# Two products behind a gated attention on one core: block 0 passes all six weight units before block 1, the plan's DMA costs and the addresses of the matmul operands change

## The chip, the core and the metric

The kernel runs on one core of a Trainium2 chip. A core has TensorE (PE, matmuls), VectorE (DVE), ScalarE (ACT), GpSimd (POOL) and SyncE (SP, which here issues nearly all DMAs). Each engine runs its own instructions in order and waits for others on semaphores. SBUF is the on-chip memory of 128 partitions, PSUM the accumulators that PE writes. The metric is the device time of one execution in microseconds, lower is better.

## The reference

```
def attention(q, k, v, alpha):              # B, H, S, D = 4, 8, 768, 48
    state = zeros(B, H, D, D)
    for t in range(S):
        state = alpha[:, :, t, :, None] * state + einsum('bhd,bhe->bhde', k[:, :, t], v[:, :, t])
        y[:, :, t] = einsum('bhd,bhde->bhe', q[:, :, t], state)
    return y

x = attention(...).transpose(0, 2, 1, 3).reshape(3072, 384)
x = ((x @ w_a) * (x @ w_b)) @ w_out         # 384 -> 1536 -> 384
h = x @ w_in                                # 384 -> 2048
return (max(h, 0) + beta * min(h, 0)) @ w_out2      # -> 384
```

Attention's inputs and beta are float32. The weights are float64; the chip reads them as 64-bit words and makes its own parts of them.

## The kernel before

**Work and tiling.** The 3072 tokens are 24 chunks of 128 (index g), four chunks make a block of 512 tokens (index n, 0 to 5). A block's attention result x is a tile of 512 columns, held as a high and a low part (both float32r, the format that PE takes at one column a cycle). The weights are likewise split into high and low. So each product is three matmuls: high by high, low weight by high x, high weight by low x (`mm3`, lines 926, 927, 929).

The first product has six units (index u) of 256 hidden columns, each in two halves (index i = 2u + o). A half-unit of a block is `up` for w_a (9 matmuls into tile pa), `up` for w_b (9 into pb), on ACT a copy of pa to a_sb, on DVE a_sb times pb (line 1057), on ACT the high part gh (line 950), on DVE the low part gl (line 954), and two half-units later `down1` with w_o (9 matmuls into acc). The second product has 8 units and 16 half-units a block: 9 matmuls into pi, DVE for the activation, gh and gl again, 9 matmuls into acc.

**Weights.** Each raw tile (ra, rb, ro; 768 KB) is loaded once and split by `conv`: five DVE operations of 768 columns and two ACT ones for each of the tiles, ending with line 453. Unit 0's tiles go partly over PE (the cl matmuls, lines 481 to 483). The second product's 16 tiles (ws) are split the same way between 200 and 430 us, stored to DRAM (w2d), and loaded back when SBUF is free.

**Attention.** Per chunk: loads of alpha (ra), of k and q (kq) and of v; on DVE two scans (lines 584 and 594, with a reciprocal of four values between them, line 590) that turn alpha into running products and their inverses, and the product kq times these (line 599); on PE scores (line 625), the chunk's own and cross terms (786, 808, 793); DVE and ACT move the state and x. The scans need a constant of ones and zeros as second operand: `ones` for the first, `invs` for the second, whose heads the reciprocal overwrites. From block 2 on (`BY_BLOCKS`) the keys are turned by DVE and by DRAM: `turn` (line 660) transposes 32 x 32 squares into kt, four DMAs store it to ktd (`away`, line 664), four load it back as ks (`back`, line 674). Kt and ks share one buffer (tag ks).

**What sets the order.** Operations are first entered in a graph with a duration, a latency and a key, and then ordered for all engines by a planner (`Graph.place`, `latest`, `search`): a list scheduler with a random search over the keys; its result is the order in which the instructions are written. The keys come from `at`, the planned start of each half-unit in the order of `SEGMENTS`, and for chunks of later blocks from `block_at[n] - (BC - c) * 12000 - 14000` in nanoseconds. `SEGMENTS` lists (block, first unit, end unit): blocks 0 and 1 pass units 0 to 2 each, then units 3 to 5 each, then the other blocks pass six. Where a block is left half-way its sums are copied to a tile part by ACT and added later by DVE (`evict1`). `SPLIT` names the (block, unit) whose matmuls are cut into two halves of 256 columns, so that they can start when two chunks are there. `fill` writes idle matmuls (wp) into planned gaps at the beginning.

**Addresses.** Tiles are laid out pool by pool in the order in which the pools are opened. The program has weights at 192 and x, gh and gl at 256 bytes past a multiple of 512.

Of the kernel before, what the change touches and what calls it, by code (L numbers as in the profile page):

```python
# [14 lines left out]
F32 = mybir.dt.float32  # L15
BF16 = mybir.dt.bfloat16
# [4 lines left out]
ALU = mybir.AluOpType  # L21
# [4 lines left out]
P = 128  # L26
CH = 128
HC = CH // 2
BC = 4
MB = BC * CH  # L30
SQ = 32
BT = P // SQ

SEGMENTS = (
    (0, 0, 3), (1, 0, 3), (0, 3, 6), (1, 3, 6),
    (2, 0, 6), (3, 0, 6), (4, 0, 6), (5, 0, 6),
)
LAG = 2
SPLIT = ((0, 0), (1, 0))
BY_BLOCKS = 2  # L40

ON_PE = (("a", 0), ("b", 0), ("o", 0))

# [2 lines left out]
HOP = 250  # L46
LEAD = {"DVE": 80, "ACT": 90}
T_MOE = 30000
STRETCH = 1.2
URGENT = 40000  # L50
PAUSE = 500
SLACK = 500
# [16 lines left out]
class Graph:  # L69
# [11 lines left out]
    def add(self, eng, dur, fn, key, deps=(), lat=0, after=(), pool=None, burst=False, line=None):  # L81
        o = Op()
        o.pool, o.hold, o.burst = pool, [], burst
        o.eng, o.dur, o.fn, o.key, o.lat = eng, dur - LEAD.get(eng, 0), fn, key, lat + LEAD.get(eng, 0)
        o.users, o.soft, o.n = [], [], len(self.ops)
        for d in {x.n: x for x in deps if x is not None}.values():
            d.users.append(o)
        for d in {x.n: x for x in after if x is not None}.values():
            d.soft.append(o)
        if line:  # L90
            if line in self.last and self.last[line] not in [x for x in after if x is not None]:
                self.last[line].soft.append(o)
            self.last[line] = o
        self.ops.append(o)
        return o
# [203 lines left out]
def body(tc, akq, v, vg, w_a, w_b, w_o1, w_in, w_o2, beta, out):  # L299
    nc = tc.nc  # L300
# [5 lines left out]
    NJ = H // 2  # L306
    D = KT * P // H
    GR = 64 - D
    NA = NJ * (CH + 1) + 1
    NC = NJ * CH  # L310
    NB = NG // BC

    with ExitStack() as ctx:
        ctx.enter_context(tc.manual_schedule())
        pool = lambda name, bufs=1, **k: ctx.enter_context(tc.tile_pool(name=name, bufs=bufs, **k))
        const, wpool, pers = pool("const"), pool("wpool"), pool("pers")
        xpool, cpool, gpool, tp = pool("xpool", 2), pool("cpool", 2), pool("gpool", 2), pool("tp", 2)
        dram = pool("dram", space=DRAM)
        ps_mm, ps_acc = pool("ps_mm", 2, space=PSUM), pool("ps_acc", space=PSUM)
        ps_att = pool("ps_att", space=PSUM)  # L320
# [4 lines left out]
        ident = plus.bitcast(F32)  # L325
        mask = const.tile([P, P], F32, name="mask")
        betaT = const.tile([P, F2], F32, name="betaT")
        ones = pers.tile([P, NJ, CH + 1], F32, name="ones")
        invs = pers.tile([P, NJ, CH + 1], F32, name="invs")
        Z = pers.tile([P, BC, NJ, D], F32, name="Z")  # L330
        At = pers.tile([P, 2 * NC], F32, name="As")
        x2d = [dram.tile([P, 2, KT, MB], F32, name=f"x2d{n}") for n in range(NB)]
        w2d = [dram.tile([P, 2 * UC], F32, name=f"w2d{i}") for i in range(2 * NU2)]
        ktd = [dram.tile([SQ, NJ, BT, P], F32, name=f"ktd{g}") for g in range(NG)]


        warm = ones.bitcast(BF16)[:, 0, 2 : 2 + 2 * CH]

        def fill(t0, t1):
            wp = ps_mm.tile([P, MB // 2], F32, name="wp", tag="mm")  # L340
            for _ in range(int((t1 - t0) * 0.7) // 110):
                nc.tensor.matmul(wp, warm[:, 0:P], warm, start=True, stop=True)

        nc.gpsimd.memset(ones, 0.0)
        nc.gpsimd.memset(ones[:, :, 0:1], 1.0)
        nc.gpsimd.memset(invs, 0.0)
        make_identity(nc, eye)
        nc.gpsimd.memset(mask, 1.0)
        nc.gpsimd.affine_select(
            out=mask, in_=mask, pattern=[[1, P]], compare_op=ALU.is_ge, fill=0.0,  # L350
# [10 lines left out]
        whole, parts = slice(0, MB), (slice(0, MB // 2), slice(MB // 2, MB))  # L361
        flat = [(n, 2 * u + o, s, t) for s, (n, u0, u1) in enumerate(SEGMENTS) for u in range(u0, u1)
                for t in (parts if (n, u) in SPLIT else (whole,)) for o in range(2)]
        span = lambda t: MM if t == whole else MM // 2 + 10
# [4 lines left out]
        due, block_at = {}, {}  # L369
# [131 lines left out]
        for u in range(NU1):  # L501
            for nm, src in (("a", w_a), ("b", w_b), ("o", w_o1)):
                x = nm, u
# [16 lines left out]
        st = [dict() for _ in range(NG)]  # L520
        xt, xuse, xdone, xpart = {}, {}, {n: [] for n in range(NB)}, {}
        xring, lring, rring, vring = Ring(2), Ring(2), Ring(2), Ring(2)
        aring, kring, sring = Ring(1), Ring(1), Ring(1)
        both = ps_att.tile([P, 2, 2 * NC // 2], F32, name="both")
        yfree, afree = [], []
        att = lambda nm: ps_att.tile([P, NJ, CH], F32, name=nm, tag="att")
        before = {"scan": None}
        accfree = [[] for _ in range(KT)]
        state = [[] for _ in range(BC)]
        sums = [At[:, NC + i * NJ * D : NC + (i + 1) * NJ * D].rearrange("p (j d) -> p j d", d=D) for i in range(2)]  # L530
        slots = [Z[:, c] for c in range(BC)] + sums[1:]

        def place(g):
            n, c = divmod(g, BC)
            key = c * 1000 - 100000 if n == 0 else block_at[n] - (BC - c) * 12000 - 14000
            if n == 1:
                key = block_at[n] - (BC - c) * 9500 - 6000

            def A(eng, dur, fn, deps, early=0, lat=0, after=(), line=None):
                return G.add(eng, dur, fn, key - early, deps, lat, after, burst=eng == "PE", line=line)  # L540

            return st[g], n, c, n == 0, A

        def inputs(g):
            s, n, c, start, A = place(g)
# [28 lines left out]
            kT = lambda: s["kq"][:, 0]  # L574
            qT = lambda: s["kq"][:, 1]
            r0 = lambda: s["ra"][:, 0 : NA - 1].rearrange("p (j t) -> p j t", j=NJ)[:, :, 0:1]
            la = A("SP", 1000 if g == 0 else 720, load_a, rwait, 14000, 2400 if g == 0 else 3000, line="ra")
# [5 lines left out]
            def scan_r():  # L583
                nc.vector.tensor_tensor_scan(
                    out=s["ra"][:, 0 : NA - 1][:, ::-1], data0=s["ra"][:, : NA - 1 : -1],
                    data1=ones.rearrange("p j t -> p (j t)"), initial=0.0, op0=ALU.mult, op1=ALU.add,
                )

            def recip():
                nc.vector.reciprocal(invs[:, :, 0:1], r0())  # L590

            def scan_a():
                a = s["ra"][:, NA - 1 : 2 * NA - 2]
                nc.vector.tensor_tensor_scan(out=a, data0=a, data1=invs.rearrange("p j t -> p (j t)"),
                                             initial=0.0, op0=ALU.mult, op1=ALU.add)

            def mul():
# [1 line left out]
                nc.vector.tensor_tensor(out=s["kq"], in0=s["kq"], in1=f[:, :, :, 1:], op=ALU.mult)  # L599

            turned = n >= BY_BLOCKS
            r = A("DVE", 1220, scan_r, [la])
            rc = A("DVE", 180, recip, [r, before["scan"]])
            sa = before["scan"] = A("DVE", 1220, scan_a, [rc])
            slack = SLACK if not start else 0
            k1 = q1 = A("DVE", 1220, mul, [lq, sa], 0, slack)
            rhold.append(k1)
# [33 lines left out]
        def chunk(g):  # L641
            s, n, c, start, A = place(g)
# [3 lines left out]
            kT, qT, r0, r, k1, lv = (s[x] for x in ("kT", "qT", "r0", "r", "k1", "lv"))  # L646
            spare, rhold, lhold, slack = (s[x] for x in ("spare", "rhold", "lhold", "slack"))
            ahead = st[g + 1] if n > 1 and g + 1 < NG else None
            turned = n >= BY_BLOCKS

# [5 lines left out]
                slots[c], slots[BC] = new, old  # L656

            def turn():
                s["kt"] = tp.tile([P, NJ, P], F32, name="kt", tag="ks", bufs=1)
                nc.vector.transpose(s["kt"], kT())  # L660

            def away(b):
                def f():
                    nc.sync.dma_start(
                        ktd[g].rearrange("t j a f -> t (j a) f")[:, :, b * SQ : (b + 1) * SQ],
                        s["kt"][b * SQ : (b + 1) * SQ].rearrange("p j (a d) -> p (j a) d", d=SQ),
                    )
                return f

            def back(a):  # L670
                def f():
                    if a == 0:
                        s["ks"] = tp.tile([P, NJ, P], F32, name="ks", tag="ks", bufs=1)
                    nc.sync.dma_start(s["ks"][a * SQ : (a + 1) * SQ], ktd[g][:, :, a, :])
                return f

            if turned:
                x = A("DVE", 650, turn, [k1, *kring.take()])
                lhold.append(x)
                moved = [A("SP", 430, away(b), [x], 0, 2000) for b in range(BT)]  # L680
                x = None
                back_at = []
                for a in range(BT):
                    x = A("SP", 350, back(a), moved, 0, 3800, after=[x])
                    back_at.append(x)

            zs = None
# [16 lines left out]
            if start:  # L704
# [3 lines left out]
                x = A("PE", 560, s["keys"], [k1, *w0])  # L708
                pa = A("PE", 1120, s["scores"], [k1, *w1, *w2])
            elif "front" in s:  # L710
                x = pa = s["front"]
            elif turned:
                x = pa = A("PE", 630, s["both"], [k1, *afree, *yfree])
            else:
                x = pa = A("PE", 1150, s["both"], [k1, *aring.take(), *afree, *yfree])
                khold = aring.last()
            if turned:
                ks = back_at
            else:
                ks = [A("ACT", 600, ev_k, [x, *kring.take()])]  # L720
# [131 lines left out]
            if start:  # L852
# [3 lines left out]
                x = A("ACT", 360, kept, [ds])  # L856
# [175 lines left out]
        def down1(k):  # L1032
            n, i, s, t = flat[k]
            _, u0, u1 = SEGMENTS[s]
            key = at[k + LAG] + 18 * MM
# [6 lines left out]
        for k, (n, i, s, t) in enumerate(flat):  # L1042
            u, o = divmod(i, 2)
            x = lambda n=n: xt[n]
            b = {}
# [31 lines left out]
        for k in range(2 * NU2):  # L1077
            b = {}
            key = t0 + k * (t1 - t0) // (2 * NU2)
            _, c = conv((w_in, w_o2)[k % 2][k // 2], f"s{k % 2}", f"s{k % 2}", key,  # L1080
                        [stored[k - 2]] if k >= 2 else part_users[k], lambda r, b=b: b.update(r=r))
# [10 lines left out]
        for k in range(2 * NU2):  # L1092
            x = "id"[k % 2], k // 2
# [55 lines left out]
        for k, (n, i) in enumerate(flat2):  # L1149
# [3 lines left out]
            b = {}  # L1153
            p, m, bh = up(at2[k], [done["i", u], ld], lambda n=n: xt[NB + n], ("i", u), o)
# [95 lines left out]
```

## Time and profile before

| | us |
|---|---|
| median of 3 runs | 943.03 |
| lowest, highest | 941.46, 948.37 |
| the profiled execution | 943.25 |
| its span, first to last instruction | 941.5 |
| PE busy in the span | 932.5 |
| DVE busy | 564.0 |
| ACT busy | 245.2 |

Matmuls overlap, so PE's busy time says that it nearly always has one under way, not that it is at its peak. What one matmul costs is the distance from its start to the next one's. An engine's idle time in a window is the window less its busy time.

### The profile page before, as it was taken

The page shows a single profiled execution, that of the slowest core. Times are in us where ns is not written, and L with a number is a line of the kernel's source. Part 1 is how long each engine was busy: PE and PEld are TensorE (multiplying, and loading weights), DVE is VectorE, ACT ScalarE, POOL GpSimd, SP SyncE. Part 2 cuts the span into 40 slices and gives each one's busy share as a digit, 9 for nine tenths or more (in the row PEclk, how much of TensorE's full clock was granted, in tenths as well). Part 3 has the DMA queues.
Part 4 walks back from the last instruction along what each step waited for, and adds up shares of the span by engine and source line. Part 5 has one row for each costly group of instructions (what it writes and reads, how often), then busy time and mean ns, then how long its engine had stood idle before and what let it go on. Part 6 is the DMA issues. An engine that isn't in the chain of part 4 may idle for free.

```text
span 941.5 us, 15646 instructions
## 1 busy us (share of the span) xinstructions
PE 932.5 (99%) x6637; PEld 760.1 (81%) x6637; DVE 564.0 (60%) x865; ACT 245.2 (26%) x406; POOL 2.2 (0%) x11
## 2 busy tenths in 40 slices
PE   9999999999999999999999999999999999999998
PEld 7788887888888788787888888888888888888886
DVE  8999964674886687663232264554545545545554
ACT  3555531223333333331122121111111111111111
POOL 0000000000000000000000000000000000000000
PEclk9999999999999999999999999999999999999999
DMA  9973103563657767763266620100200200200000
GB/s 353 403 262 102 32 1 79 159 189 137 210 162 228 249 207 217 241 175 93 82 235 202 212 91 1 68 34 1 89 12 1 101 1 0 101 1 1 34 0 34
DMA packets 75238, 112.89 MB, mean 120 GB/s; under 512 B 38689, under 2 KB 48417, under 8 KB 75169
## 3 DMA queue, kind: packets, MB, share of 16 engines
q1 hardware_dynamic: 75024, 111.77, 36.1%
q8 instruction: 52, 0.85, 0.4%
q14 instruction: 18, 0.14, 0.0%
q10 hardware_dynamic: 144, 0.13, 0.0%
HBM read 78.97 MB, written 30.93 MB: 117 GB/s over the span
## 4 chain that ended last, share of the span: by engine, by line
PE 90%; DVE 5%; DMA 2%; issue 1%; SPq 1%; ACT 0%; DVEq 0%; ACTq 0%
PE acc L926 12%; PE acc L929 12%; PE acc L927 12%; PE pi L926 7%; PE pi L927 7%; PE pi L929 7%; PE pb L926 5%; PE pa L926 5%; PE pb L927 5%; PE pa L929 5%; PE pa L927 5%; PE pb L929 5%; PE both L786 2%; PE both L625 1%; DMA v<-in_v 1%; DMA ra<-in_akq 1%
## 5 line engine op out<-in xcount | busy, mean ns | idle before, releaser
L950 ACT CAST gh<-ng 128x512 fp32r<-128x512 f32 x96 | 59.5, 620 | 329.8 <-DVE ng L1163 274.0
L1159 DVE TENSOR_SCALAR ng<-pi,betaT 128x512 f32<-128x512 f32 x96 | 72.1, 751 | 105.6 <-PE pi L929 104.7
L954 DVE TENSOR_TENSOR gl<-ng,gh 128x512 fp32r<-128x512 f32 x96 | 66.3, 690 | 79.6 <-ACT gh L950 79.6
L926 PE MATMUL pi<-x,v 128*128 128x512 f32 x288 | 113.3, 393 | 0.0
L929 PE MATMUL acc<-gl,v 128*128 128x512 f32 x288 | 113.1, 393 | 0.0
L926 PE MATMUL acc<-gh,v 128*128 128x512 f32 x288 | 112.9, 392 | 0.0
L927 PE MATMUL pi<-x,v 128*128 128x512 f32 x288 | 112.7, 391 | 0.0
L927 PE MATMUL acc<-gh,v 128*128 128x512 f32 x288 | 112.1, 389 | 0.0
L1057 DVE TENSOR_TENSOR a_sb<-a_sb,pb 128x512 f32<-128x512 f32 (+1 forms) x76 | 49.9, 656 | 83.3 <-PE pb L929 83.3
L926 PE MATMUL pb<-x,wb 128*128 128x512 f32 (+1 forms) x228 | 87.8, 388 | 0.6 <-DVE a_sb L1057 0.6
L926 PE MATMUL acc<-gh,wo 128*128 128x512 f32 (+1 forms) x228 | 88.4, 388 | 0.0
L926 PE MATMUL pa<-x,wa 128*128 128x512 f32 (+1 forms) x228 | 87.3, 386 | 0.0
L929 PE MATMUL acc<-gl,wo 128*128 128x512 f32 (+1 forms) x228 | 86.8, 381 | 0.0
L927 PE MATMUL pb<-x,wb 128*128 128x512 f32 (+1 forms) x228 | 86.0, 380 | 0.5 <-DVE wb L453 0.5
L927 PE MATMUL acc<-gh,wo 128*128 128x512 f32 (+1 forms) x228 | 86.4, 379 | 0.0
L927 PE MATMUL pa<-x,wa 128*128 128x512 f32 (+1 forms) x228 | 85.9, 380 | 0.0
L950 ACT CAST gh<-a_sb 128x512 fp32r<-128x512 f32 (+1 forms) x76 | 45.3, 596 | 140.8 <-DVE a_sb L1057 131.5
L929 PE MATMUL pi<-x,v 128*128 128x512 f32 x288 | 81.6, 391 | 0.0
L1054 ACT COPY a_sb<-pa 128x512 f32<-128x512 f32 (+1 forms) x76 | 42.7, 562 | 107.1 <-PE pa L929 106.9
L1163 DVE SCALAR_TENSOR_TENSOR ng<-pi,ng 128x512 f32<-128x512 f32 x96 | 66.3, 691 | 3.1
L926 PEld LDWEIGHTS pi<-x,v 128*128 128x128 f32 x288 | 54.1, 188 | 13.7 <-DVE ng L1163 2.1
L954 DVE TENSOR_TENSOR gl<-a_sb,gh 128x512 fp32r<-128x512 f32 (+1 forms) x76 | 50.1, 659 | 25.0 <-ACT gh L950 24.9
(126 smaller groups left out, 1360.3 us busy)
## 6 DMA issues: line engine op xcount, KB each, us to landing
kq<-in_akq SPq DMA_DIRECT2D x24, 512.0 KB, 5.1
w2d<-ws SPq DMA_DIRECT2D x16, 768.0 KB, 5.1
v<-w2d SPq DMA_DIRECT2D x16, 768.0 KB, 5.9
x2d<-x SPq DMA_DIRECT2D x18, 512.0 KB, 3.7
x<-x2d SPq DMA_DIRECT2D x6, 1536.0 KB, 6.9
ra<-in_akq SPq DMA_DIRECT2D x24, 258.5 KB, 3.9
v<-in_v SPq DMA_DIRECT2D x24, 256.0 KB, 5.0
rs<-in_w_in SPq DMA_DIRECT2D x8, 768.0 KB, 6.0
```

The lines of the kernel that those rows point to most:

```text
L625: nc.tensor.matmul(a[hs, i, j, :], kT()[ps, j, hs], qT()[ps, j, hs], start=True, stop=True, skip_group_check=True)
L786: nc.tensor.matmul(y_of(k, half(p), part_of(h)), s["v"][part_of(h), 2 * j + i, :], s["As"][part_of(h), i, j, :], start=first, stop=False, ...
L926: nc.tensor.matmul(o, lh, rh, start=first and n == 0, stop=False)
L927: nc.tensor.matmul(o, ll, rh, start=False, stop=False)
L929: nc.tensor.matmul(o, lh, rl, start=False, stop=last and n == len(pairs) - 1)
L950: nc.scalar.copy(gq[idx][0], src())
L954: nc.vector.tensor_tensor(out=gl, in0=src(), in1=gh.bitcast(F32), op=ALU.subtract)
L1054: nc.scalar.copy(b["a"], ba["t"])
L1057: nc.vector.tensor_tensor(out=b["a"], in0=b["a"], in1=bb["t"], op=ALU.mult)
L1159: nc.vector.tensor_scalar(out=b["n"], in0=bh["t"], scalar1=0.0, scalar2=betaT[:, i : i + 1], op0=ALU.min, op1=ALU.mult)
L1163: nc.vector.scalar_tensor_tensor(out=b["n"], in0=bh["t"], scalar=0.0, in1=b["n"], op0=ALU.max, op1=ALU.add)
```

## The change

`SEGMENTS` becomes one entry a block, with all six units; nothing is copied to part any more. Only block 0's first unit is still cut in halves. In the plan the DMAs of kt and ks go from 430 and 350 ns to 640 each, with a longer latency, and every SP operation whose key is over 110 us gets 3.5 us of latency more; chunks of blocks 2 to 5 are 16 us apart in the keys. One tile `heads` takes the place of ones and invs: the reciprocal overwrites its four heads, and GpSimd writes ones back (`begin`) before the next chunk's first scan. Kt gets room of its own behind the tile As. Pools are opened in another order and a tile of 320 bytes is put into the constants; with that weights, x, gh and gl begin at multiples of 512 bytes.

```diff
-SEGMENTS = (
-    (0, 0, 3), (1, 0, 3), (0, 3, 6), (1, 3, 6),
-    (2, 0, 6), (3, 0, 6), (4, 0, 6), (5, 0, 6),
-)
+SEGMENTS = tuple((n, 0, 6) for n in range(6))
-SPLIT = ((0, 0), (1, 0))
+SPLIT = ((0, 0),)
+PACE = 16000
+STEADY, SPARE = 110000, 3500
+PAD = 80
-STRETCH = 1.2
+STRETCH = 1.1
...
+        lat += SPARE if eng == "SP" and key > STEADY else 0
...
-        const, wpool, pers = pool("const"), pool("wpool"), pool("pers")
-        xpool, cpool, gpool, tp = pool("xpool", 2), pool("cpool", 2), pool("gpool", 2), pool("tp", 2)
+        const, wpool, xpool = pool("const"), pool("wpool"), pool("xpool", 2)
+        cpool, gpool, tp, pers = pool("cpool", 2), pool("gpool", 2), pool("tp", 2), pool("pers")
...
-        ones = pers.tile([P, NJ, CH + 1], F32, name="ones")
-        invs = pers.tile([P, NJ, CH + 1], F32, name="invs")
+        const.tile([P, PAD], F32, name="pad")
-        At = pers.tile([P, 2 * NC], F32, name="As")
+        At = pers.tile([P, NC + 2 * NJ * D + NC], F32, name="As")
+        heads = pers.tile([P, NJ, CH + 1], F32, name="heads")
...
+        kt = At[:, NC + 2 * NJ * D :].rearrange("p (j t) -> p j t", j=NJ)
...
-            key = c * 1000 - 100000 if n == 0 else block_at[n] - (BC - c) * 12000 - 14000
+            key = c * 1000 - 100000 if n == 0 else block_at[n] - (BC - c) * PACE - 14000
...
-                nc.vector.reciprocal(invs[:, :, 0:1], r0())
+                nc.vector.reciprocal(heads[:, :, 0:1], r0())
+
+            def begin():
+                nc.gpsimd.memset(heads[:, :, 0:1], 1.0)
...
-            r = A("DVE", 1220, scan_r, [la])
-            rc = A("DVE", 180, recip, [r, before["scan"]])
-            sa = before["scan"] = A("DVE", 1220, scan_a, [rc])
+            r = A("DVE", 1220, scan_r, [la, before["scan"]])
+            rc = A("DVE", 180, recip, [r])
+            sa = A("DVE", 1220, scan_a, [rc])
+            before["scan"] = A("POOL", 110, begin, [sa])
...
-                x = A("DVE", 650, turn, [k1, *kring.take()])
+                x = A("DVE", 700, turn, [k1, *tring.take()])
                 lhold.append(x)
-                moved = [A("SP", 430, away(b), [x], 0, 2000) for b in range(BT)]
-                x = None
+                moved = [A("SP", 640, away(b), [x], 0, 3500) for b in range(BT)]
+                tring.use(*moved)
+                held, x = kring.take(), None
...
-                    x = A("SP", 350, back(a), moved, 0, 3800, after=[x])
+                    x = A("SP", 640, back(a), [*moved, *held], 0, 5000, after=[x])
```

Where unit 3 begins, on PE (a name's digit is the unit, x_331 and x_357 are block 0's x, x_737 block 1's). Before:

```order
L929 MATMUL pb_1707<-x_737,wb2_1009 128x512 x3
L926 MATMUL pa_1720<-x_331,wa3_1260 128x512
L927 MATMUL pa_1720<-x_331,wa3_1260 128x512
L926 MATMUL pa_1720<-x_331,wa3_1260 128x512
L927 MATMUL pa_1720<-x_331,wa3_1260 128x512
```

The same place now, which stands some 200 rows earlier on PE:

```order
L934 MATMUL acc2_692<-gl_1062,wo2_999 128x512
L791 MATMUL both_154<-As_96,v_667 64x64 x8
L798 MATMUL both_154<-kq_572,Z_95 48x64 x8
L798 MATMUL both_154<-kq_572,As_96 48x64 x8
L931 MATMUL pa_1142<-x_357,wa3_1006 128x512
```

Before, block 0 takes up wa3 after block 1 has passed wb2; now it goes on from its own unit 2, with a chunk of block 1's attention between.

At the start, on DVE (scans and reciprocals of the first chunks; the product kq closes a chunk's part). Before:

```order
L584 SCALAR_TENSOR_TENSOR ra_156<-ra_156,ones_94 128x516
L590 RECIPROCAL invs_95<-ra_156 128x4
L584 SCALAR_TENSOR_TENSOR ra_158<-ra_158,ones_94 128x516
L594 SCALAR_TENSOR_TENSOR ra_156<-ra_156,invs_95 128x516
L590 RECIPROCAL invs_95<-ra_158 128x4
L599 TENSOR_TENSOR kq_160<-kq_160,ra_156 128x1024
```

Now:

```order
L585 SCALAR_TENSOR_TENSOR ra_155<-ra_155,heads_97 128x516
L591 RECIPROCAL heads_97<-ra_155 128x4
L598 SCALAR_TENSOR_TENSOR ra_155<-ra_155,heads_97 128x516
L603 TENSOR_TENSOR kq_157<-kq_157,ra_155 128x1024
L585 SCALAR_TENSOR_TENSOR ra_159<-ra_159,heads_97 128x516
```

The second chunk's first scan stood between the first chunk's two; now it stands behind both and the product.

Near the end of the attention, on SP (ktd22 is the store of the last chunk but one; the kq below it is the last chunk's load). Before:

```order
L664 DMA ktd22_142<-kt_4689 512x1x32 x4
L674 DMA ks_4754<-ktd22_142 32x4x128 x4
L565 DMA kq_4774<-in_akq 128x1024
L569 DMA v_4778<-in_v 128x512
L1084 DMA w2d15_119<-ws1_4711 128x1536
```

Now:

```order
L668 DMA ktd22_142<-As_96 512x1x32 x4
L566 DMA kq_4615<-in_akq 128x1024
L570 DMA v_4620<-in_v 128x512
L678 DMA ks_4655<-ktd22_142 32x4x128 x4
L668 DMA ktd23_143<-As_96 512x1x32 x4
```

The loads of kq and v have moved ahead of the four loads of ks, and the last store of a ws tile is earlier in the queue.

## Rows read from the trace of the kernel before

**Rows 1.** The page: engines, DVE in 40 slices of the span, the chain by engine.

```profile
PE 932.5 (99%) x6637; PEld 760.1 (81%) x6637; DVE 564.0 (60%) x865; ACT 245.2 (26%) x406; POOL 2.2 (0%) x11
...
DVE  8999964674886687663232264554545545545554
...
PE 90%; DVE 5%; DMA 2%; issue 1%; SPq 1%; ACT 0%; DVEq 0%; ACTq 0%
```

**Rows 2.** Windows: stretch, length, busy us of PE, PEld, DVE, ACT, POOL, clock, DMA share.

```profile
30.00:60.00 30.00, 28.89 (x422) 24.14 (x421) 29.50 (x56) 16.79 (x31) 0.00 (x0) 1.00 0.89 344
...
360.00:400.00 40.00, 39.34 (x273) 31.61 (x271) 29.66 (x47) 14.02 (x22) 0.00 (x0) 1.00 0.70 219
400.00:440.00 40.00, 37.97 (x441) 30.16 (x439) 20.45 (x31) 10.55 (x17) 0.00 (x0) 1.00 0.56 158
```

**Rows 3.** PE in order of time near 471 us: start, length; nine matmuls lie between the starts.

```profile
470.86 0.39 PE L926 MATMUL acc<-gh,wo 128*128 128x512 f32 x1
...
472.92 0.39 PE L926 MATMUL pb<-x,wb 128*128 128x512 f32 x1
```

**Rows 4.** The same near 23 us, 256 columns; five matmuls lie between the starts.

```profile
23.04 0.28 PE L927 MATMUL pa<-x,wa 128*128 128x256 f32 x1
...
23.63 0.51 PE L929 MATMUL pa<-x,wa 128*128 128x256 f32 x3
```

**Rows 5.** SP, DVE and PE in order of time, 415 to 431 us; brackets: idle before.

```profile
414.98 3.35 SPq L664 DMA_DIRECT2D ktd<-kt  x4
420.00 2.50 SPq L674 DMA_DIRECT2D ks<-ktd  x4
422.54 0.59 SPq L565 DMA_DIRECT2D kq<-in_akq  x1
...
427.51 1.22 DVE L599 TENSOR_TENSOR kq<-kq,ra 128x1024 f32<-128x1024 f32 x1 [4.30 <-DMA kq<-in_akq]
428.65 0.68 DVE L1057 TENSOR_TENSOR a_sb<-a_sb,pb 128x512 f32<-128x512 f32 x1
...
430.25 0.46 PE L786 MATMUL both<-As,v 64*64 64x64 f32 x16 [2.03 <-DVE As L813]
```

**Rows 6.** DVE and PE in order of time, 380 to 385 us.

```profile
380.33 1.23 DVE L584 TENSOR_TENSOR_SCAN ra<-ra,ones 128x516 f32<-128x516 f32 x1 [4.15 <-DMA ra<-in_akq]
...
384.59 0.50 PE L926 MATMUL pb<-x,wb 128*128 128x512 f32 x1 [0.64 <-DVE a_sb L1057]
```

**Rows 7.** The tile part: DVE's adds, duration min/median/max in ns, first and last start.

```profile
L996 DVE TENSOR_TENSOR part<-part,acc x6: 677/680/682, 176.9 to 223.9; 128x512 f32<-128x512 f32 x6
```

**Rows 8.** In order of time: unit 5's last tile on DVE and PE, wa3 on PE.

```profile
130.22 0.95 DVE L453 SCALAR_TENSOR_TENSOR wo<-c,c 128x768 fp32r<-128x768 int32 x1
...
167.81 0.39 PE L926 MATMUL acc<-gh,wo 128*128 128x512 f32 x1
...
123.45 0.39 PE L926 MATMUL pa<-x,wa 128*128 128x512 f32 x1
```

**Rows 9.** DVE's groups by form, 0 to 132 us: busy us, mean ns, idle before.

```profile
L584 DVE TENSOR_TENSOR_SCAN ra<-ra,ones 128x516 f32<-128x516 f32 x12 | 14.6, 1224 | 3.6 <-DMA ra<-in_akq 3.6
...
L954 DVE TENSOR_TENSOR gl<-a_sb,gh 128x256 fp32r<-128x256 f32 x8 | 3.3, 418 | 0.0
...
L690 DVE TENSOR_TENSOR Z<-Z,ra 128x192 f32<-128x192 f32 x7 | 2.5, 359 | 0.0
```

**Rows 10.** GpSimd in order of time: the write of four heads.

```profile
1.38 0.10 POOL L345 MEMSET ones<- 128x4 f32 x1
```

**Rows 11.** PE's 384-column groups: three pieces (28 us), one run (40 us).

```profile
28.17 0.91 PE L481 MATMUL cl<-c,plus 128*128 128x384 f32 x2
...
29.10 0.33 PE L483 MATMUL cl<-wb,plus 128*128 128x384 f32 x1
...
39.95 0.91 PE L481 MATMUL cl<-c,plus 128*128 128x384 f32 x2
...
40.87 0.81 PE L483 MATMUL cl<-c,plus 128*128 128x384 f32 x2
```

More of the change, by code (lines that the diff above doesn't have):

```diff
@@ L334, in body @@
         ktd = [dram.tile([SQ, NJ, BT, P], F32, name=f"ktd{g}") for g in range(NG)]
-        warm = ones.bitcast(BF16)[:, 0, 2 : 2 + 2 * CH]
+        warm = heads.bitcast(BF16)[:, 0, 2 : 2 + 2 * CH]
         def fill(t0, t1):
@@ L342, in fill @@
                 nc.tensor.matmul(wp, warm[:, 0:P], warm, start=True, stop=True)
-        nc.gpsimd.memset(ones, 0.0)
-        nc.gpsimd.memset(ones[:, :, 0:1], 1.0)
-        nc.gpsimd.memset(invs, 0.0)
+        nc.gpsimd.memset(heads, 0.0)
+        nc.gpsimd.memset(heads[:, :, 0:1], 1.0)
         make_identity(nc, eye)
@@ L522, in body @@
         xring, lring, rring, vring = Ring(2), Ring(2), Ring(2), Ring(2)
-        aring, kring, sring = Ring(1), Ring(1), Ring(1)
+        aring, kring, sring, tring = Ring(1), Ring(1), Ring(1), Ring(1)
         both = ps_att.tile([P, 2, 2 * NC // 2], F32, name="both")
@@ L585, in scan_r @@
                     out=s["ra"][:, 0 : NA - 1][:, ::-1], data0=s["ra"][:, : NA - 1 : -1],
-                    data1=ones.rearrange("p j t -> p (j t)"), initial=0.0, op0=ALU.mult, op1=ALU.add,
+                    data1=heads.rearrange("p j t -> p (j t)"), initial=0.0, op0=ALU.mult, op1=ALU.add,
                 )
             def recip():
-                nc.vector.reciprocal(invs[:, :, 0:1], r0())
+                nc.vector.reciprocal(heads[:, :, 0:1], r0())
+            def begin():
+                nc.gpsimd.memset(heads[:, :, 0:1], 1.0)
             def scan_a():
                 a = s["ra"][:, NA - 1 : 2 * NA - 2]
-                nc.vector.tensor_tensor_scan(out=a, data0=a, data1=invs.rearrange("p j t -> p (j t)"),
+                nc.vector.tensor_tensor_scan(out=a, data0=a, data1=heads.rearrange("p j t -> p (j t)"),
                                              initial=0.0, op0=ALU.mult, op1=ALU.add)
@@ L658, in turn @@
             def turn():
-                s["kt"] = tp.tile([P, NJ, P], F32, name="kt", tag="ks", bufs=1)
-                nc.vector.transpose(s["kt"], kT())
+                nc.vector.transpose(kt, kT())
             def away(b):
@@ L665, in f @@
                         ktd[g].rearrange("t j a f -> t (j a) f")[:, :, b * SQ : (b + 1) * SQ],
-                        s["kt"][b * SQ : (b + 1) * SQ].rearrange("p j (a d) -> p (j a) d", d=SQ),
+                        kt[b * SQ : (b + 1) * SQ].rearrange("p j (a d) -> p (j a) d", d=SQ),
                     )
```

## The prediction

> **What bounds the kernel now.** I read the page's table of engines first, then its chain, then windows by stage, and the instructions in order of time at the places where TensorE (PE) waits. PE is busy 99% of the span and carries 90% of the chain [rows 1]; the granted clock is 1.00 in every stretch that I looked at [rows 2], the upper of the two levels, 2.4 GHz. So the time is PE's own work plus its few waits. The work is 512-column matmuls: nine take 2.06 us from start to start, 0.229 us each [rows 3]; half-width ones start every 0.118 us [rows 4]. By the code there are 27 for each of 68 undivided half-units of the first product and 18 for each of 96 of the second, 3564 in all, 816 of the 941.5 us; the rest is attention, 216 half-width matmuls, warm-up, the last store, and waits.
>
> The waits are small. From 30 to 60 us PE lacks 1.1 of 30 us, from 360 to 440 us it lacks 2.7 of 80 [rows 2], together 3.8. Two waits make the second figure. At 430.25 PE had stood 2.03 us for VectorE (DVE): DVE runs in order, and had itself stood 4.30 us for the load of kq, with PE's next operand queued behind. That load left SyncE's queue (SP) only at 422.54, after four stores of the turned keys (3.35 us) and four loads of them (2.50 us) [rows 5]. At 384.59 it is the same with a load of ra, 4.15 us on DVE and 0.64 on PE [rows 6].
>
> To carry on: DVE has slack as a whole (60%), but none up to 118 us, where its five digits are 8 and 9; the sixth is 6 [rows 1].
>
> **The change part by part**, against the profiled execution: 943.25 us, its span 941.5 and 1.75 around it. The median of the runs is 943.03, so nothing needs to be rescaled.
>
> *One split less.* Block 1's first unit is no longer cut in halves: 108 half-width matmuls become 54 wide ones, 54 x 0.229 - 108 x 0.118 = **-0.4 us**, all of it on PE.
>
> *Six units in a row.* The partial sums of blocks 0 and 1 go: six copies on ScalarE and six adds on DVE. The adds ran from 176.9 us on [rows 7], where DVE is not the bound, so nothing is taken for them. What it costs is slack. Before, the last weight tile of unit 5 was finished on DVE at 130.22 + 0.95 = 131.2 us and first used at 167.81: 36.6 us to spare [rows 8]. Now PE comes to it early. In the new order the same attention work stands ahead of its first use as stood ahead of wa3 before (PE there at 123.45), with 45 more wide and 108 fewer half-width matmuls: 123.45 + 45 x 0.229 - 108 x 0.118 = 121.0 us. DVE has 22 rows fewer ahead of that tile: six of the long kind (scans and the kq product, 1.22 us, about 1.14 from start to start, since the next one begins 0.08 to 0.09 before the end [rows 5]), eight half-width ones (0.42, so 0.33) and eight short ones (decays of 0.36, so 0.27, which I take for all eight): 6.84 + 2.64 + 2.16 = 11.6 us [rows 9]. It finishes at 131.2 - 11.6 = 119.6. So 1.4 us remain where 36.6 were: PE is fed, just. Bounds: nothing, if DVE never stands, and 3 us, if it stands once for a load as it did for 4.15 us [rows 6]. I take **+1.0**, nearer the low end since the loads of this stage are issued ahead of need.
>
> *First units.* Ahead of the first wide product DVE now has two rows more (rows 1 to 30 of the new order in place of 1 to 28): one scan (1.14) and one decay (0.27) fewer, five conversion steps of unit 0 more, half-width and so taken at 0.33 to 0.47, 1.8 together: **+0.4 us**, between 0 and 1.5, the latter if the scan is on the path all the same.
>
> *One constant for both scans.* The ones and the reciprocals share a tile, so the next chunk's scan waits until GpSimd has written four ones back. That write takes 0.10 us [rows 10]. In the new order at least one other DVE row stands between the two scans at all 23 places, most often eleven or more; the tightest has the kq product, as long as a scan. Cost 0; without that cover the write's 0.10 a place, or an estimated 0.4 if each of the two hand-overs takes one and a half times as long again, and eight of the places lie where DVE has no slack: 3 us at most.
>
> *Later DMAs counted longer; the turned keys in a buffer of their own.* The plan's costs for the eight small DMAs of a chunk go from 0.43 and 0.35 us to 0.64 each; the trace has 3.35 us for four [rows 5]. In the new order the second to last kq load stands behind the stores but ahead of the loads of the turned keys, and chunks are 16 us apart instead of 12 in the plan's keys. Nothing of the work changes; what can be won is the 2.7 us that PE stood between 360 and 440 us. Bounds: 0 (SP still stands at the first store whose data is late, with the rest of its queue behind) and -2.7; I take **-2.4**, since both waits have the cause that is corrected. What is late next: the conversion of the second product's weights, which has all the time to 540 us.
>
> *Operands at 0 modulo 512.* Weights move from 192 and x, gh, gl from 256 past a multiple of 512 to 0. This touches every wide matmul, 3618 of them after the change: 1 ns of pitch is 3.6 us. At 2.4 GHz 512 columns are 213.3 ns, and the pitch is 229, so 15.6 ns of each are something else. No row shows an operand at 0. The nearest rows are matmuls of 384 columns whose moving operand is, once, three separate pieces of 512 bytes at 192 past the boundary, each of them across it, and once one run of 1536 bytes: from the first matmul of the group to the last it is 0.93 and 0.92 us [rows 11]. So crossings cost nothing that can be seen, and half the length has not half the excess: 118 - 106.7 = 11.3 ns. It looks like a cost of the instruction, not of the address. Bounds: -15.6 ns each (-56 us) and, as a read that now meets another in the same place, +3 ns (+11 us). I take **0**, by those rows. Hence the Trainium skill, "SBUF — State Buffer", section "SBUF: two separate sides": only the pair of ports that VectorE and GpSimd share is contended, PE never waits there. By it the term is 0 too, but no run here can show that. Against it stands the Trainium skill, "TensorE: Matmul & The Clock Gate", section "Wait — 56ns, not 53.3ns?": warm matmuls of 512 columns start every 215.7 ns, a fixed 2.5 ns over the columns. The trace disagrees by 13 ns; by that page alone the sum would be an estimated 48 us lower.
>
> Sum: 943.25 - 0.4 + 1.0 + 0.4 + 0 - 2.4 + 0 = **941.9 us**.
>
> **The rivals.** *A, the addresses are part of the 15.6 ns.* For it: an excess that the columns don't explain, and every operand of these matmuls off the boundary. Against it: [rows 11], and a pitch that is the same in both products although their weights and blocks lie elsewhere. Its middle case takes away the part that grows with length: (15.6 - 11.3) x 2 = 8.6 ns, 3618 x 8.6 = 31 us, **911 us**; its ends are 2.6 ns (932) and all of it (886).
>
> *B, DVE becomes the bound of the first 120 us.* Slower. It decides from 1.4 us on: each further microsecond that DVE stands ahead of unit 5's last tile is one of PE's. Three waits of the size seen at 380 and 427 us (4.15, 4.30 and 4.15 again) make 12.6 - 1.4 = 11.2 in place of the 1.0 taken: **952 us**. For it: weights of all six units and the attention loads now compete in the stage where the queues are fullest. Against it: in the first 120 us DVE stood only 3.6 us for a load, its first [rows 9].
>
> *C, the longer DMA costs do nothing*, because SP still stands in order: 2.4 us less gain, **944 us**; that is inside the forecast's case.
>
> **How the numbers follow.** About 1%, 9.4 us, is what a measurement of this kernel tells from no change. Forecast with C: 0.65, its own range 938 to 947. A: 0.25, spread from 886 to 932. B: 0.10, from 948 to 956. Faster by over 1% is A, 0.25; slower is B, 0.10; within is 0.65. From 914 to 951 leaves out the lower part of A, 0.25 x 28/46 = 0.15, and half of B, 0.05.
>
> **What would show it.** The pitch of nine wide matmuls in the second product: 2.06 us by the forecast, 1.98 by A's middle. PE's idle time from 360 to 440 us: under 0.5 us; as much as before by C. DVE busy without a break to about 120 us, unit 5's last tile ready near 120 us and PE there within a microsecond or two; long stands of PE between 60 and 120 us would be B. After 540 us nothing should differ but by A. The prediction is wrong if the pitch moves by 3 ns or more, or if DVE waits for loads in the first 120 us.

## The result and the profile after

The kernel after takes 932.44 us (median of 4 runs, 932.32 to 932.57), the kernel before 942.25 us beside it (median of 4, 941.25 to 948.37). The ratio is 0.989, 95% interval 0.987 to 0.991: faster by 1.1%, 9.8 us, where 941.9 us was forecast. The profiled execution went from 943.25 to 932.32 us, its span from 941.5 to 930.6.

The page of the kernel after, its table of engines and the shares of the chain:

```profile
PE 925.4 (99%) x6585; PEld 757.0 (81%) x6585; DVE 560.5 (60%) x855; ACT 242.6 (26%) x396; POOL 7.0 (1%) x34
...
PE 97%; DVE 1%; DMA 1%; issue 1%; ACT 0%; DVEq 0%; ACTq 0%
```

PE is the bound as before [rows 1], with 97% of the chain in place of 90%. Its busy time fell by 7 us (932.5 to 925.4) although it computes the same products: so more than waits is gone. The busy time of TensorE and the others by stage, after (PE, PEld, DVE, ACT, POOL, clock, DMA share, GB/s):

```profile
30.00:60.00 30.00, 29.94 (x282) 25.57 (x281) 30.00 (x54) 16.97 (x32) 0.98 (x3) 1.00 1.01 400
...
90.00:120.00 30.00, 30.00 (x323) 23.88 (x321) 30.00 (x47) 14.13 (x21) 0.54 (x2) 1.00 0.26 75
...
360.00:400.00 40.00, 40.00 (x452) 32.43 (x451) 21.01 (x32) 10.15 (x18) 0.21 (x2) 1.00 0.48 127
400.00:440.00 40.00, 40.00 (x348) 32.39 (x348) 13.43 (x20) 8.12 (x14) 0.00 (x0) 1.00 0.16 41
```

In the three stretches of [rows 2] PE lacked 1.11, 0.66 and 2.03 us; now it lacks 0.06, 0 and 0. That is the first part of the gain. The second stands in a stretch where nothing was moved: windows from 560 to 920 us, in the second product, PE alone (busy us, count of its matmuls, clock, DMA share, GB/s), of the kernel before

```profile
560.00:920.00 360.00, 360.00 (x1569) 1.00 0.08 29
```

and of the kernel after.

```profile
560.00:920.00 360.00, 359.98 (x1583) 1.00 0.08 29
```

PE has no wait in either, the granted clock is the same, and yet 14 more matmuls of the same kind pass in the same 360 us. Call the distance from one wide (512-column) matmul's start to the next one's the pitch. Its mean over all pairs of wide matmuls in succession that start under 260 ns apart (3468 pairs before, 3516 after) is 229.0 ns before and 227.2 after. Over 3618 wide matmuls 1.8 ns is **6.5 us**. With the 3.8 us of PE's waits (4.0 us of gaps in PE before, 0.2 after) that makes 10.3 of the 10.9 us. The remaining 0.6 is what is left of small terms: summed from start to start without gaps, all wide and half-width matmuls together take 7.2 us less, so 0.7 more than the pitch explains, the warm-up takes 0.5 more, and the other matmuls 0.4 less.

The waits went where they came from. DVE's waits for loads, from the view of waits, before:

```profile
DVE kq L599 <- DMA kq<-in_akq: 27.4, 10, 5.4
DVE ra L584 <- DMA ra<-in_akq: 10.4, 5, 4.2
```

and after (us in total, times, longest):

```profile
DVE ra L585 <- DMA ra<-in_akq: 3.8, 1, 3.8
...
DVE kq L603 <- DMA kq<-in_akq: 0.3, 1, 0.3
```

Only the first load, which nothing can precede, is still waited for by more than 0.3 us. In order of time after, on SP the last of the 24 kq loads:

```profile
399.43 0.47 SPq L566 DMA_DIRECT2D kq<-in_akq  x1
```

and on DVE the row that reads it:

```profile
408.22 1.22 DVE L603 TENSOR_TENSOR kq<-kq,ra 128x1024 f32<-128x1024 f32 x1
```

The load leaves 8.8 us ahead of its reader, which has no wait in brackets. Before, 4.97 us lay between the same two, and 4.30 of these DVE stood [rows 5].

Last, unit 5's final weight tile on DVE after, and PE's first use of it:

```profile
118.76 0.93 DVE L453 SCALAR_TENSOR_TENSOR wo<-c,c 128x768 fp32r<-128x768 int32 x1
```

```profile
120.09 0.50 PE L931 MATMUL acc<-gh,wo 128*128 128x512 f32 x1
```

Ready at 119.7 us, used at 120.1: the spare 36.6 us of [rows 8] are down to 0.4, and PE doesn't wait.

### The profile page after: what moved, and what is told of

Same layout as the page of the kernel before. It is cut to its first block, busy times and chain, and to the rows that moved or that the text cites. A ratio compares the mean times of both kernels' runs of the same rounds, so it can differ in the third digit from the quotient of the medians.

```text
span 930.6 us, 15550 instructions
## 1 busy us (share of the span) xinstructions
PE 925.4 (99%) x6585; PEld 757.0 (81%) x6585; DVE 560.5 (60%) x855; ACT 242.6 (26%) x396; POOL 7.0 (1%) x34
## 4 chain that ended last, share of the span: by engine, by line
PE 97%; DVE 1%; DMA 1%; issue 1%; ACT 0%; DVEq 0%; ACTq 0%
PE acc L931 13%; PE acc L934 12%; PE acc L932 12%; PE pi L931 7%; PE pi L932 7%; PE pi L934 7%; PE pa L931 6%; PE pb L931 5%; PE pa L932 5%; PE pa L934 5%; PE pb L932 5%; PE pb L934 5%; PE both L791 2%; PE both L630 1%; PE both L813 1%; PE both L798 1%
## 5 line engine op out<-in xcount | busy, mean ns | idle before, releaser
L931 PE MATMUL acc<-gh,wo 128*128 128x512 f32 (+1 forms) x222 | 86.9, 391 | 0.0
L931 PE MATMUL pb<-x,wb 128*128 128x512 f32 (+1 forms) x222 | 86.5, 391 | 0.0
L932 PE MATMUL acc<-gh,wo 128*128 128x512 f32 (+1 forms) x222 | 85.3, 384 | 0.0
L932 PE MATMUL pb<-x,wb 128*128 128x512 f32 (+1 forms) x222 | 85.0, 384 | 0.0
L932 PEld LDWEIGHTS acc<-gh,v 128*128 128x128 f32 x288 | 54.1, 188 | 11.3
```

Source lines behind the costliest of these rows:

```text
L931: nc.tensor.matmul(o, lh, rh, start=first and n == 0, stop=False)
L932: nc.tensor.matmul(o, ll, rh, start=False, stop=False)
```

## The experiments

All are edits of the kernel after unless said otherwise. "Gaps" is the time in which PE had no instruction running, summed from its first one on (4.0 us before, 0.2 after); "pitch" the mean defined above. Where one time is given without a range, it is of one execution; its granted clock was 1.00. Two questions were open: what changed the pitch, and what took the waits away.

### The pitch: which address matters?

The theory is that the start addresses set the pitch; the rival, that it came with the new plan, whose matmuls have other neighbours in time.

**All at 192.** The pad tile goes, so that the pools slip back by 320 bytes.

```diff
-        const.tile([P, PAD], F32, name="pad")
```

> The kernel after without its pad tile: weights, x, gh and gl all begin at 192 modulo 512 bytes; plan and instructions are those of the kernel after. Theory address (the start address sets the pitch of the wide matmuls): the mean pitch goes back from 227.2 ns to about 229.0, which over 3618 wide matmuls is 6.5 us, so about 939 us, with PE's idle still near 0.2 us. Theory plan (the pitch came with the new order of work and other neighbours in time, not with addresses): pitch 227.2 ns and 932.4 us, as the kernel after.

Measured: 932.98 us (932.96 to 933.5), ratio to before 0.990 (0.987 to 0.993), pitch 227.2 ns. The theory in this form falls: with no operand at 0 the pitch is as good.

**Moving operands at 256.** A matmul's two operands are the weights, which are loaded first, and the moving operand (x, gh or gl). A tile of 64 floats stands between the weights' pool and x's pool; all that lies behind it moves too:

```diff
-        const, wpool, xpool = pool("const"), pool("wpool"), pool("xpool", 2)
+        const, wpool, between, xpool = pool("const"), pool("wpool"), pool("between"), pool("xpool", 2)
+        between.tile([P, 64], F32, name="gap")
```

> Weights begin at 0 modulo 512 bytes, x, gh and gl (the moving operands) at 256; nothing else differs from the kernel after. Theory moving operand: pitch about 229.0 ns and about 939 us. Theory weights (the operand that is loaded into the array): 227.2 ns and 932.4 us. Theory plan: 227.2 ns.

Measured: 932.83 us, pitch 227.2 ns. By itself this spoke for the plan.

**Weights at 192.** The pad of 80 floats moves behind the weights, into the same pool `between`; the pad of the constants goes.

```diff
-        const.tile([P, PAD], F32, name="pad")
+        between.tile([P, PAD], F32, name="gap")
```

> Weights begin at 192 modulo 512 bytes, x, gh and gl at 0; nothing else differs from the kernel after. Theory moving operand: pitch 227.2 ns and 932.4 us. Theory weights: about 229.0 ns and 939 us. Theory plan: 227.2 ns.

Measured: 939.42 us, pitch 229.0 ns, on the plan of the kernel after. So the plan isn't it, and neither is the weights' address alone, since 192 was good in the first experiment.

**All at 256.**

```diff
-PAD = 80
+PAD = 16
```

> Weights, x, gh and gl all begin at 256 modulo 512 bytes. If the address matters modulo 256 or less: pitch 227.2 ns and 932.4 us. If it matters modulo 512: about 229.0 ns and 939 us. Theory plan: 227.2 ns.

Measured: 933.05 us, pitch 227.2 ns. The four results fit one rule, formed here: what matters is how far the moving operand begins from the weights, modulo 256. Distance 0 (192 and 192, 0 and 256, 256 and 256, 0 and 0) gives 227.2; distance 64 (weights 192, moving operand 256, the kernel before; or 192 and 0, the third experiment) gives 229.0. The rule was tested by the next two.

**Distance 128.** The gap of the second experiment with 32 floats, so weights at 0 and x, gh, gl at 128.

> Weights begin at 0 modulo 512 bytes, x, gh and gl at 128; nothing else differs from the kernel after. So far the mean pitch was 227.2 ns with weights and moving operands at 192 and 192, 256 and 256, 0 and 256, 0 and 0, and 229.0 with 192 and 0, and 192 and 256. Theory distance (the pitch depends on how far weights and moving operands lie apart) modulo 128 or less: 227.2 ns, 932.8 us. Theory distance modulo 256: over 228 ns, 936 to 939 us. Theory that any start at a multiple of 64 is good for the moving operand when the weights begin at 0: 227.2 ns.

Measured: 951.52 us, pitch 232.7 ns: 19 us more than after, and worse than before. Distance modulo 256 is the theory that is left, but its 936 to 939 us were far too low: it says that 128 differs from 0, not by how much. The same window as above:

```profile
560.00:920.00 360.00, 360.00 (x1543) 1.00 0.08 29
```

1543 matmuls where the kernel after passes 1583.

**The kernel before with equal addresses.** The edit is to the kernel before; only the order of its pools changes, and all operands begin at 192 (the attention's tiles move too).

```diff
-        const, wpool, pers = pool("const"), pool("wpool"), pool("pers")
-        xpool, cpool, gpool, tp = pool("xpool", 2), pool("cpool", 2), pool("gpool", 2), pool("tp", 2)
+        const, wpool, xpool = pool("const"), pool("wpool"), pool("xpool", 2)
+        cpool, gpool, tp, pers = pool("cpool", 2), pool("gpool", 2), pool("tp", 2), pool("pers")
```

> The kernel before with its pools in the order of the kernel after (pers last), so that weights, x, gh and gl all begin at 192 modulo 512 bytes; plan, instructions and PE's waits are those of before. Theory distance (weights and moving operands at the same place modulo 256): pitch 227.2 ns, 3618 matmuls by 1.8 ns is 6.5 us, so about 935.5 us, with PE idle still about 4 us. Theory plan (the pitch came with the new plan): 229.0 ns and 942 us.

Measured: 937.83 us (937.04 to 938.98) against 943.12 beside it, ratio 0.995 (0.993 to 0.997); the span is 6.2 us shorter. Pitch 227.2 ns, gaps 3.8 us. Its window:

```profile
560.00:920.00 360.00, 359.98 (x1583) 1.00 0.08 29
```

This is the count of the kernel after, with the plan of before: the addresses alone are worth 6.2 us by the spans, 5.3 by the medians.

**Only gh and gl at 128.** The gap stands between the pools of c and of gh, gl, so that x stays at 0. "First product" in the expectation means the matmuls that read x (into pa, pb and pi), "second product" those that read gh and gl (into acc, in both halves of the kernel).

```diff
-        cpool, gpool, tp, pers = pool("cpool", 2), pool("gpool", 2), pool("tp", 2), pool("pers")
+        cpool, between, gpool = pool("cpool", 2), pool("between"), pool("gpool", 2)
+        tp, pers = pool("tp", 2), pool("pers")
+        between.tile([P, 32], F32, name="gap")
```

> As the kernel after, but only gh and gl, the moving operands of the second product, begin at 128 modulo 512 bytes; weights and x, the moving operand of the first product, begin at 0. Theory distance (it is the two operands of a matmul that count): first product 227.2 ns, second product about 232.7 ns as with 128 in both; 1728 matmuls by 5.5 ns, 9.5 us more than after, about 942 us. Theory that one misplaced operand slows the engine as a whole, or that x alone counts: both products at one pitch, 232.7 or 227.2 ns, and 951 or 932.4 us.

Measured: 943.93 us, the span 11.6 us longer than after. The matmuls into acc have a pitch of 232.9 ns, as with 128 in both. There are 1494 wide ones (the expectation's 1728 counts other matmuls), and 5.9 ns each over the 227.0 of after make 8.8 of the 11.6 us. Those that read x should have stayed at 227.2. Of each nine the last three, of high weights by low x, did (227.2, 227.6 and 227.0 ns from one of them to the next, for pa, pb and pi); from one to the next of the first six it is 230.3, 228.0 and 230.7, where the kernel after has 227.7, 227.8 and 227.1. In order of time:

```profile
600.14 0.39 PE L933 MATMUL pi<-x,v 128*128 128x512 f32 x1
...
601.53 0.84 PE L936 MATMUL pi<-x,v 128*128 128x512 f32 x3
602.21 0.40 PE L933 MATMUL acc<-gh,v 128*128 128x512 f32 x1
...
604.30 0.39 PE L933 MATMUL pi<-x,v 128*128 128x512 f32 x1
```

Here six matmuls into pi with high x take 1.39 us, 0.232 each; its three with low x 0.68, 0.227 each; the nine into acc 2.09, 0.232 each. So the distance between the two operands of one matmul is not the whole of it: the six are slower although theirs is 0.

The slow ones are those that come right behind a group into acc. By the group ahead of them, the first five steps of a group of nine have these means (in brackets the kernel after): pa behind acc 231.3 ns (226.8), pi behind acc 231.5 (226.7), but pa behind pb 227.1 (227.2) and pb behind pa 226.7 (226.7). The later steps of the groups behind acc are as after again: 227.1 for pa, 226.7 for pi. So nine matmuls whose operands lie 128 apart slow about five good ones behind them. Writes beside them are not needed: those of the five steps that have no instruction of DVE, ACT or POOL beside them take 230.4 ns for pa and 231.3 for pi (226.6 and 226.7 after). Why the pace carries over stays open.

### The waits: costs, units, or the luck of the search?

**The old DMA costs**, addresses and units as after:

```diff
-PACE = 16000
-STEADY, SPARE = 110000, 3500
+PACE = 12000
+STEADY, SPARE = 110000, 0
...
-                x = A("DVE", 700, turn, [k1, *tring.take()])
+                x = A("DVE", 650, turn, [k1, *tring.take()])
-                moved = [A("SP", 640, away(b), [x], 0, 3500) for b in range(BT)]
+                moved = [A("SP", 430, away(b), [x], 0, 2000) for b in range(BT)]
-                    x = A("SP", 640, back(a), [*moved, *held], 0, 5000, after=[x])
+                    x = A("SP", 350, back(a), [*moved, *held], 0, 3800, after=[x])
```

> The kernel after with the planner's old costs of the transposed tiles' DMAs and of the later loads (PACE 12000, SPARE 0, away 430 and 2000, back 350 and 3800, turn 650); units, tiles and addresses stay as after. Theory longer costs (they took PE's two waits between 360 and 440 us away): these waits come back, PE idle rises from 0.2 to about 2.9 us, and the time from 932.4 to about 935 us, pitch 227.2 ns. Theory no part of the costs (the waits went with the other order of units or with the tile of its own for the turned keys): PE idle stays below 0.6 us, and the time at 932.4 us.

Measured: 937.4 us (936.92 to 938.95), ratio to before 0.995 (0.993 to 0.997), gaps 3.8 us, pitch 227.2 ns. DVE's and PE's waits in this kernel, and the DVE row behind the longest of PE's:

```profile
DVE kq L603 <- DMA kq<-in_akq: 17.7, 10, 2.9
DVE ra L585 <- DMA ra<-in_akq: 5.1, 2, 3.7
```

```profile
PE pb L931 <- DVE a_sb L1062: 2.6, 2, 2.3
```

```profile
280.89 1.23 DVE L603 TENSOR_TENSOR kq<-kq,ra 128x1024 f32<-128x1024 f32 x1 [2.68 <-DMA kq<-in_akq]
```

The waits are back, of the same kind (PE for a DVE row that stands behind a late kq load), but the long one is near 281 us and not at 428. The time rises by 5.0 us, of which the gaps are 3.6; the rest isn't explained.

**The old order of units**, with costs and addresses of after:

```diff
-SEGMENTS = tuple((n, 0, 6) for n in range(6))
+SEGMENTS = (
+    (0, 0, 3), (1, 0, 3), (0, 3, 6), (1, 3, 6),
+    (2, 0, 6), (3, 0, 6), (4, 0, 6), (5, 0, 6),
+)
-SPLIT = ((0, 0),)
+SPLIT = ((0, 0), (1, 0))
-STRETCH = 1.1
+STRETCH = 1.2
```

> The kernel after with the old order of units (blocks 0 and 1 in turn, three units each), both splits and STRETCH 1.2; costs, tiles and addresses stay as after. Theory of the prediction (six units in a row cost 1.0 us, later first units 0.4, the split saved 0.4): about 931.4 us. Theory from the two traces (six units in a row took PE's waits of 1.1 us between 30 and 60 us away, and the split 0.4): about 934 us, PE idle about 1.3 us, pitch 227.2 ns in both.

Measured: 935.02 us (934.69 to 935.18), ratio to before 0.992 (0.990 to 0.993), gaps 1.2 us, nearly all before 80 us. Neither theory's number is met, though the second has the sign right. So six units in a row don't cost 1.0 us; on this draw of the search, the split and STRETCH included, they gain 2.6 (2.3 by the spans).

A planner with a random search can make such differences by chance. Three runs asked for that. **Another seed**, all costs as after:

```diff
-SEED, TRIES, WORLDS = 2, 1500, 2
+SEED, TRIES, WORLDS = 3, 1500, 2
```

> The kernel after with another seed of the planner's random search, all costs as after. Theory costs (the longer DMA costs and the order of units take PE's waits away, whatever the search finds): PE idle below 1 us and 932 to 933 us. Theory luck (the plan of the kernel after is one good draw among many): PE idle of 2 to 4 us and 934.5 to 937 us.

Measured: 933.73 us (933.54 to 934.29), gaps 1.5 us, nearly all before 50 us. Neither theory's numbers: the plan after is a good draw by 1.3 us, not by 2 to 4. **The old DMA costs under that seed**:

> The kernel with the old DMA costs of the experiment before, under another seed of the search. Theory costs: PE idle again 2.5 us or more and 935 us or more, as with the first seed (3.8 us and 937.4). Theory luck: it could lie anywhere from 932.4 to 938 us, and no higher than the kernel after with the other seed.

Measured: 934.43 us (933.32 to 938.71), gaps 1.9 us, all but 0.1 of them after 130 us. Again neither theory's number: less idle time than by costs, and later than the kernel after with this seed, which luck had as its upper end. Against the other costs with this seed that is 0.7 us, where it was 5.0 with the first: the price in time depends on the draw, and here the spread of the runs covers it. The waits of DVE that the costs are meant for don't depend on it. With the new costs and the other seed DVE waits once for a load, 3.6 us for its first; with the old ones there are these rows.

```profile
DVE kq L603 <- DMA kq<-in_akq: 12.0, 8, 3.0
DVE ra L585 <- DMA ra<-in_akq: 9.1, 5, 3.6
```

**Only the turned keys' costs put back** (the last three pairs of lines of the diff with the old DMA costs; PACE and SPARE stay as after, seed 2):

> The kernel after with only the costs of the turned keys' stores and loads put back (turn 650, away 430 and 2000, back 350 and 3800); PACE 16000 and SPARE 3500 of the later loads stay. Theory turned keys (the loads queued late behind stores counted too short): PE's waits come back, idle 2.5 us or more, about 936 us. Theory later loads (earlier keys and 3.5 us of spare for SP's loads are enough): PE idle below 1 us and 932 to 933.5 us.

Measured: 932.94 us (932.26 to 933.42), gaps 1.2 us, of which 1.1 before 20 us. DVE's waits for loads:

```profile
DVE ra L585 <- DMA ra<-in_akq: 4.1, 2, 3.6
DVE kq L603 <- DMA kq<-in_akq: 0.2, 1, 0.2
```

This kernel and that with all the old costs differ by PACE and SPARE alone: DVE's waits for loads fall from 22.8 to 4.3 us in sum, and the time from 937.4 to 932.94. So PACE and SPARE suffice on this seed: loads planned 3.5 us earlier than they need, and chunks 16 us apart. Which of the two does it wasn't separated, and the turned keys' own buffer stands in all these runs. Beside that, the higher costs of the stores and loads of the turned keys show no more than 0.5 us (932.44 against 932.94), with PE's gaps outside the first 20 us as small as after. Of all these kernels none is faster than the kernel after.

## Why the prediction was right, and where it was wrong

The range of 914 to 951 held, but by a rival and not by the forecast. The prediction gave 0.65 to a time within 1% of before and 0.25 to A, faster by more; A's case came, and the time lies 9.5 us under the forecast, outside its own 938 to 947. That A's lower end is 932 is partly luck: it takes 2.6 ns off every wide matmul, and measured are 1.8 ns and 2.4 us more won from waits than forecast. By the steps:

**What bounds the kernel**: right. PE's work and its waits are the time, and each part of the gain is one of these two.

**Operands at 0 modulo 512**, taken at 0: this is the step that failed, by 6.5 us. Its error is in the row that was taken for the nearest. [rows 11] compare 384-column matmuls whose moving operand crosses boundaries or doesn't; what counts is the distance to the other operand, which these rows don't vary. Nor did the equal pitch of both products tell against A: their operands lay at the same places modulo 512. From "crossings cost nothing that can be seen" the text went to "a cost of the instruction, not of the address"; but a difference of 1.8 ns in 229 can't be seen in starts printed to 10 ns, and the count of matmuls in a long window would have been the view for it. Rival A was the right mechanism at the low end of its range (2.6 ns, 932 us, against 1.8 ns measured), and its reason is refuted: not the boundary of 512, since everything at 192 is as fast. The bound above zero, "a read that now meets another in the same place", had its reason the wrong way round: the same place modulo 256 is the best one tried. There is a loss, but at a distance of 128, 3.7 ns over the kernel before. And the sign that was set, a pitch moved by 3 ns or more, was too coarse: 1.8 ns alone take the sum to 935.4, out of the forecast's own range.

**Later DMAs counted longer**, -2.4 with bounds 0 and -2.7: the waits of 2.7 us between 360 and 440 us are gone, and the mechanism was right (a load queued late on SP, DVE behind it, PE behind DVE). What does it, on the seed that was tried, is PACE and SPARE, not the longer costs of the turned keys, with which the working began. (The load that moved ahead of the loads of the turned keys is the last kq load, not the second to last: it is the one at 399.43 above.) The size is one draw's: undone with one seed it costs 5.0 us, with another 0.7. Rival C, no gain because SP still stands in order, is refuted by the waits of DVE on both seeds; of the turned keys' costs taken alone it was right.

**Six units in a row**, +1.0: the working of slack was right within a microsecond (tile ready at 119.6 forecast, 119.7 measured; PE there at 121.0 forecast, 120.1 measured), its price wrong: DVE never stands for a load ahead of that tile, so the lower bound of 0 applied. Also PE's waits of 1.1 us between 30 and 60 us, which the sum left in place, went; undoing units, split and STRETCH together costs 2.6 us. How much of that is the order and how much the draw wasn't separated. Rival B is refuted by the same rows.

**One split less**, -0.4, and **one constant for both scans**, 0: nothing contradicts them (0.7 us of wide and half-width matmuls are left beside the pitch), neither was tried alone. The view of waits names no wait of DVE for GpSimd's write. **First units**, +0.4: the first pa starts at 24.75 us where it started at 22.82, but PE has attention work meanwhile and no wait; what is lost is 0.5 us of warm-up matmuls (81, 11.66 us from start to start, where there were 79, 11.19).

So 2.4 + 0.4 - 1.0 - 0.4 = 1.4 us of gain were forecast and 10.9 found in the profiled execution: 6.5 from the term taken as 0, and 3.8 of waits where 2.4 - 1.0 was counted.

## What to carry to other kernels

Where PE is the bound and its matmuls are all alike, count them in a long window without waits: a nanosecond of pitch that no single row shows is microseconds in the sum, and here the distance modulo 256 bytes between weights and moving operand was worth 6 us by an order of pools, and 19 us are lost where it falls on 128. Before an address change is priced, the trace row for it must vary the same thing, both operands' places, and not one operand's. And a change of a planner's costs is judged by the waits that it is meant for, over two seeds of its search; a single time mixes it with the draw.

## What the runs showed of the hardware that was not expected

The pitch of warm 512-column float32r matmuls (granted clock 1.00, 2.4 GHz), each with a weight load of its own, depends on where the moving operand begins relative to the weights: 227.2 to 227.3 ns at a distance of 0 modulo 256 bytes (ten kernels, with seven different plans), 229.0 at 64 (two kernels), 232.7 at 128 (one kernel). A distance of 192 and steps under 64 weren't tried, and why the distance matters no run here shows. It also carries over: behind nine matmuls at 128, the first five steps of a group at 0 took 231.3 and 231.5 ns in the mean, and the later ones 227.1 and 226.7 (pa and pi, with gh and gl alone at 128). At distance 0 there remain 13.9 ns over the 213.3 of 512 columns.
